# Linear attention and a cosine feed-forward layer: two more chunks paired, and Strassen's seven products in the second product of the pairs

## The chip, the core and the metric

One core of a Trainium2 chip runs the whole kernel. The metric is the time of one execution in microseconds (us) on the device. TensorE (PE) does matrix products, VectorE (DVE) and ScalarE (ACT) work elementwise, GpSimd (POOL) does a little of the attention, and SyncE (SP) issues nearly all transfers between the device memory (DRAM) and the core's buffers.

## The reference

```python
def phi(x):                                   # 64 -> 256 features
    proj = einsum('bhsd,df->bhsf', x, w_phi)
    proj = proj - max(abs(proj), axis=-1)
    return concatenate([exp(proj), exp(-proj)])
q_p, k_p = phi(q), phi(k)                     # 8 batches, 8 heads, 576 rows of 64
kv, z = einsum('bhsf,bhsd->bhfd', k_p, v), sum(k_p, axis=2)
attn = einsum('bhsf,bhfd->bhsd', q_p, kv) / (einsum('bhsf,bhf->bhs', q_p, z) + 1e-6)
x = attn as (4608 tokens, 512)
h = x @ w_in                                  # 512 x 2048
g = h * cos(h)
out = g @ w_out                               # 2048 x 512
```

The two weights arrive as float64. The kernel turns each into a high and a low part of float32; each number of x and g is split the same way, and a product of two split matrices is three products: high by high, low by high, high by low.

## The kernel before, in words

Thirty-two attention units (two heads each, `attention(u)`) write x, transposed, into `xs` and `xs_tail` in DRAM. `convert(kind, i)` makes the eight pairs of weight tiles `wi` (columns of w_in, 256 of the 2048 each) and `wo` (the same rows of w_out) and stores them to `wi_parts` and `wo_parts`. The feed-forward layer goes by chunks of 512 tokens: chunks 0 to 7 are the first 512 tokens of a batch, chunk 8 (`TAIL`) gathers the last 64 of each.

- Chunks 0 to 2 take the plain product (L969: for each tile of 128 hidden columns twelve matmuls of 512 columns), a quarter of the weights at a time, with running sums in DRAM, while the attention still runs.
- Chunks 3, 4, 5 and 6 are a `visit()` each. There the first product is Strassen's: the chunk is cut into halves of 256 tokens, the weight pair into 2 x 2 blocks, and seven block products of 256-column matmuls (L921) take the place of eight. `fold`, during chunk 3, makes the block sums of w_in that this needs. ACT copies products out of PSUM (L933), DVE adds them up (L948, L952). Then g = h cos(h) is made (ACT L991 and L999, DVE L995 and L1002), split by ACT (`gh`, L49) and DVE (`gl`, L54), and taken through the second product at once: L1018 to L1020, twelve matmuls of 512 columns a tile, with g stationary and w_out moving.
- The last two chunks, 8 and 7, go as a pair in `visit_two()`: Strassen's first product with whole chunks as halves, so its matmuls have 512 columns (L1196), 42 to a weight pair. The second product is plain (L1311 to L1313): chunk 8's at once, chunk 7's from g that was kept in buffers the attention no longer needs.

Weight pairs are read back from DRAM by `reload` where they have left their ring of buffers: three buffers for `wi`, three for `wo`.

Every instruction belongs to a `Step`, and a table of step numbers, `ORDER`, sets the order; each engine executes its own steps in that order. A step waits for the steps it depends on and for its buffers. PSUM has eight banks, given out by the same order.

Of the kernel before, what the change touches and what calls it, by code (L numbers as in the profile page):

```python
# [7 lines left out]
F32 = mybir.dt.float32  # L8
# [13 lines left out]
NSLOT = 4  # L22


@with_exitstack
def phi_attention_then_cos_ffn(ctx: ExitStack, tc: tile.TileContext, qkT, vS, w_phi, w_in, w_out, out):
# [8 lines left out]
    T = out.shape[0]  # L35
# [32 lines left out]
    class Step:  # L68
# [18 lines left out]
    ORDER = [  # L87
# [206 lines left out]
    ]  # L294
    LATENCY = dict(PE=0.35, ACT=0.25, DVE=0.2, POOL=0.25, SP=2.0)

    def plan():
# [511 lines left out]
    def visit(v):  # L809
# [94 lines left out]
        for i, pr in enumerate(pairs):  # L904
# [3 lines left out]
            if c == GROUP:  # L908
                w_fold[wi]()
# [548 lines left out]
```

## Time and profile before

| | before |
|---|---|
| median of 3 runs | 1032.85 us (1032.52 to 1035.78) |
| span of the profiled execution | 1030.4 us |
| PE busy | 1021.3 us (99%) |
| DVE busy | 760.7 us (74%) |
| ACT busy | 780.0 us (76%) |
| POOL busy | 147.1 us (14%) |
| moved by transfers | 193.39 MB |

The profile is of one execution, whose whole time isn't given apart from its span; the span is 2.45 us shorter than the median of the runs. Busy time is the time in which an engine had at least one instruction under way.

### The profile page before, as it was taken

Reading aid. Unit: us, or ns where it says so; the run is one execution under the profiler, and the core shown is the slowest. Engines: PE = TensorE matmul, PEld = TensorE weight load, DVE = VectorE, ACT = ScalarE, POOL = GpSimd, SP = SyncE. Lnnn points to the kernel's source line nnn. Section 1 sums busy time; section 2 is a strip of 40 time slices with the busy share of each in tenths; the row PEclk is TensorE's granted clock in tenths of the full one; section 3 lists DMA queues with packets and bytes.
Section 4 is the critical chain, followed back from the end, with each engine's and each line's share of the span. In section 5 each row is a group of like instructions: output and inputs, shape, how many; then the busy total and the mean of one; then the engine's idle time right before and its main releaser. Section 6 shows DMA issues by size and latency. Waiting matters only on the chain.

```text
span 1030.4 us, 23501 instructions
## 1 busy us (share of the span) xinstructions
PE 1021.3 (99%) x9402; PEld 862.9 (84%) x9402; DVE 760.7 (74%) x1426; ACT 780.0 (76%) x1592; POOL 147.1 (14%) x231
## 2 busy tenths in 40 slices
PE   9999999999999999999999999999999999999998
PEld 6778887888888788889889898888898988888886
DVE  7999888999889878988776666666666676645532
ACT  7899987778688877975889867996788875545532
POOL 3433332020200202211111110111101100000000
PEclk9999999999999999999999999999999999999999
DMA  6655665647536556774926771477347443535134
GB/s 239 212 188 161 216 203 181 219 145 257 205 115 227 189 187 222 239 225 156 328 89 227 269 269 55 164 268 256 131 163 264 141 146 83 200 126 215 41 133 153
DMA packets 86893, 193.39 MB, mean 188 GB/s; under 512 B 20608, under 2 KB 41216, under 8 KB 82944
## 3 DMA queue, kind: packets, MB, share of 16 engines
q1 hardware_dynamic: 86640, 191.82, 55.5%
q8 instruction: 74, 1.21, 0.5%
q14 instruction: 35, 0.29, 0.1%
q10 hardware_dynamic: 144, 0.07, 0.0%
HBM read 141.52 MB, written 50.33 MB: 186 GB/s over the span
## 4 chain that ended last, share of the span: by engine, by line
PE 90%; ACT 3%; DVE 3%; DMA 2%; issue 1%; POOL 0%; SPq 0%; DVEq 0%; ACTq 0%; POOLq 0%
PE bank L921 16%; PE bank L969 10%; PE bank L1018 10%; PE bank L1019 9%; PE bank L1020 9%; PE bank L1196 8%; PE bank L747 5%; PE bank L712 5%; PE bank L1312 3%; PE bank L1311 3%; PE bank L1313 3%; PE bank L608 3%; PE bank L562 2%; PE bank L654 1%; PE bank L718 1%; ACT ek L666 1%
## 5 line engine op out<-in xcount | busy, mean ns | idle before, releaser
L1018 PE MATMUL bank<-wo,gh 128*128 128x512 f32 x448 | 178.9, 399 | 0.1
L1019 PE MATMUL bank<-wo,gh 128*128 128x512 f32 x448 | 175.1, 391 | 0.0
L1020 PE MATMUL bank<-wo,gl 128*128 128x512 f32 x448 | 175.0, 391 | 0.0
L601 POOL TENSOR_TENSOR pq<-pq,bq 128x288 f32<-128x288 f32 x128 | 119.4, 965 | 165.7 <-DVE bq L597 87.2
L666 ACT ACTIVATE ek<-bank,mk 128x128 f32<-128x128 f32 x464 | 129.0, 411 | 7.0 <-DVE mk L649 6.7
L54 DVE TENSOR_TENSOR gl<-g,gh 128x512 fp32r<-128x512 f32 x128 | 89.8, 707 | 41.1 <-ACT gh L49 39.7
L1018 PEld LDWEIGHTS bank<-wo,gh 128*128 128x128 f32 x448 | 84.3, 188 | 20.7 <-issue 3.1
L995 DVE SCALAR_TENSOR_TENSOR g<-g,hs 128x512 f32<-128x512 int32 x112 | 80.1, 721 | 29.2 <-ACT g L991 24.9
L1020 PEld LDWEIGHTS bank<-wo,gl 128*128 128x128 f32 x448 | 84.1, 188 | 19.1 <-DVE gl L54 0.8
L593 POOL COPY m<-m 32x36 f32<-32x36 f32 x96 | 26.9, 280 | 506.4 <-DVE m L588 503.8
L49 ACT ACTIVATE gh<-g 128x512 fp32r<-128x512 f32 x128 | 80.8, 637 | 23.6 <-DVE g L1002 15.5
L1019 PEld LDWEIGHTS bank<-wo,gh 128*128 128x128 f32 x448 | 84.4, 188 | 14.6
L999 ACT ACTIVATE g<-g,halfpi 128x512 f32<-128x512 f32 x112 | 79.1, 719 | 18.2 <-DVE g L995 17.7
L1002 DVE TENSOR_TENSOR g<-hs,g 128x512 f32<-128x512 f32 x112 | 77.0, 691 | 16.7 <-ACT g L999 16.4
L672 ACT ACTIVATE eq<-pq 128x576 f32<-128x576 f32 x128 | 81.4, 717 | 3.7 <-POOL pq L601 3.5
L921 PE MATMUL bank<-xh_t,wi 128*128 128x256 f32 x512 | 83.6, 285 | 0.0
L921 PEld LDWEIGHTS bank<-xh_t,wi 128*128 128x128 f32 x512 | 72.5, 191 | 4.9 <-DVE wi L54 0.8
L747 PE MATMUL bank<-kv,eq 128*64 128x65 f32 x2048 | 70.4, 223 | 3.2 <-ACT hs L977 2.5
L933 ACT ACTIVATE hs<-bank 128x256 f32<-128x256 f32 x128 | 48.1, 398 | 33.5 <-PE bank L921 31.0
L747 PEld LDWEIGHTS bank<-kv,eq 128*64 128x64 f32 x2048 | 64.7, 138 | 9.5 <-ACT hs L977 2.8
L712 PEld LDWEIGHTS bank<-vs,ek 128*64 128x64 f32 x2048 | 62.5, 138 | 5.6 <-issue 1.1
L712 PE MATMUL bank<-vs,ek 128*64 128x65 f32 x2048 | 66.1, 223 | 0.0
(144 smaller groups left out, 2235.6 us busy)
## 6 DMA issues: line engine op xcount, KB each, us to landing
wi<-wi_parts SPq DMA_DIRECT2D x20, 1792.0 KB, 8.5
wo<-wo_parts SPq DMA_DIRECT2D x30, 1024.0 KB, 6.0
qk<-qkT SPq DMA_DIRECT2D x31, 640.0 KB, 5.1
wi_parts<-wi SPq DMA_DIRECT2D x32, 512.0 KB, 6.1
x_raw<-xs SPq DMA_DIRECT2D x47, 256.0 KB, 4.6
vs<-vS SPq DMA_DIRECT2D x32, 325.0 KB, 5.4
wi_raw<-w_in SPq DMA_DIRECT2D x8, 1024.0 KB, 7.0
wo_raw<-w_out SPq DMA_DIRECT2D x8, 1024.0 KB, 6.3
```

The source lines that it names most:

```text
L54: eng.tensor_tensor(out=out, in0=in_, in1=hi.bitcast(F32), op=ALU.subtract)
L601: qeng.tensor_tensor(out=d["pq"][:, c], in0=d["pq"][:, c], in1=d["bq"][:, c], op=ALU.subtract)
L666: ACT.activation(out=e[:, g, s * P:(s + 1) * P], in_=pk[:, g, :], func=AF.Exp, scale=1.0 - 2.0 * s, bias=d["lk" if s == 0 else "mk", i][:, ...
L672: ACT.activation(out=e[:, s, :], in_=d["pq"][:, j * S:(j + 1) * S], func=AF.Exp, scale=1.0 - 2.0 * s)
L712: PE.matmul(out=acc[c:c + 64, n, i, :], lhsT=e[:, s, P * n + c:P * n + c + 64], rhs=vs[b["v"].slot][:, 2 * s + i, :], start=(s == 0 and i ...
L747: PE.matmul(out=ps[64 * h:64 * h + 64, 65 * g:65 * g + 65], lhsT=d["eq", j][:, n, c:c + 64], rhs=d["kv"][:, 2 * n + j, :], start=h not in ...
L921: PE.matmul(out=out, lhsT=w[:, part, block, j * P:(j + 1) * P], rhs=d[x, name][:, j * HC:(j + 1) * HC], start=start and k == 0, stop=k == ...
L969: PE.matmul(out=bank(b), lhsT=w[:, part, 2 * r + kt // 2, kt % 2 * P:(kt % 2 + 1) * P], rhs=d.get(("from", kt), d)[x, kt], start=(k == 0), ...
L1018: PE.matmul(out=a, lhsT=gh[:, t], rhs=w[:, 0, r], start=first, stop=False)
L1019: PE.matmul(out=a, lhsT=gh[:, t], rhs=w[:, 1, r], start=False, stop=False)
L1020: PE.matmul(out=a, lhsT=gl[:, t], rhs=w[:, 0, r], start=False, stop=last)
L1196: PE.matmul(out=bank(bank_b), lhsT=w[:, part, block, j * P:(j + 1) * P], rhs=d[x, name, j], start=start and k == 0, stop=k == 5, skip_grou ...
```

## The change

Chunks 5 and 6 become a pair, ahead of the last one, so `visit()` is left with chunks 3 and 4. In both pairs the second product goes by Strassen's seven products as well, and transposed: slices of w_out are stationary and g moves. For that all g of both chunks of a pair (8 weight pairs x 4 tiles) are kept in buffers of the attention, and then seven `sweep`s go over all eight weight pairs, each into two PSUM banks: per weight pair three matmuls for each bank. Four sweeps first combine two kept tiles on DVE (`combine`). The slices of w_out come from DRAM (`fetch`, four weight pairs in one transfer of 1 MB): three sweeps take blocks of `wo_parts`, four take block sums, `wo_sums`, which `fold_wo` makes during chunk 4. The result of the pairs leaves transposed, in an output of its own, `outT`, which the host puts in place after the run.

`wi` has two buffers instead of three; the room of the third is `wi_x`, two half tiles, which a weight pair uses in the visits and x and g use in the pairs.

```diff
-    rings.update(wi=3, wo=3, v=2, ...)
+    rings.update(wi=2, wi_x=1, wo=3, v=2, ...)
...
-    kept = NP - rings["wi"]
-    TWICE = 1
-    late = [c for c in range(GROUP, NCH) if c != NCH - 2] + [NCH - 2]
+    SINGLE = (3, 4)
+    PAIRS = ((5, 6), (TAIL, 7))
+    kept = NP - rings["wi"] - rings["wi_x"]
...
+        def fold_wo():
+            def join():
+                x["t1"] = new("w_t", [P, 2 * DM], F32, "wo_s", "w_t1")
+                hi, lo = (flat(w_tiles[me][:, n]).bitcast(F32) for n in range(2))
+                DVE.tensor_tensor(out=x["t1"], in0=hi, in1=lo, op=ALU.add)
+            def sums(k):
...
+                DVE.tensor_tensor(out=o, in0=a, in1=b, op=op)
+            def sums_high():
+                x["s"] = new("w_raw", [P, 4, 2, DM // 2], F32R, "wo_st", "w_raw")
+                hi_of(ACT, x["s"][:, :, 0], x["t1"].rearrange("p (k c) -> p k c", k=4))
+            def sums_low():
+                lo_of(DVE, x["s"][:, :, 1], x["t1"].rearrange("p (k c) -> p k c", k=4), x["s"][:, :, 0])
+            def put():
+                SP.dma_start(out=wo_sums[:, i], in_=x["s"].bitcast(F32))
...
+            if c == SINGLE[-1]:
+                w_fold[wo]()
...
-            def mm2(tbs):
-                w = w_tiles[wo]
-                for tb in tbs:
-                    t = slice(tb * P, (tb + 1) * P)
-                    a = bank(c["acc"][tb])
-                    PE.matmul(out=a, lhsT=n["gh"][:, t], rhs=w[:, 0, r], start=first, stop=False)
-                    PE.matmul(out=a, lhsT=n["gh"][:, t], rhs=w[:, 1, r], start=False, stop=False)
-                    PE.matmul(out=a, lhsT=n["gl"][:, t], rhs=w[:, 0, r], start=False, stop=last)
...
+        for i, pr in enumerate(seq):
+            m, hs, whole = products(pr)
+            for r in range(2):
+                for n in range(2):
+                    wave(i, m, hs, (r, n), whole[r, n])
+            if i < NP - rings["wi"]:
+                reload("wi", seq[rings["wi"] + i], True, True)
...
+        def combine(i, o, a, b):
+            def fn():
+                DVE.tensor_tensor(out=at[(i,) + o], in0=at[(i,) + a], in1=at[(i,) + b], op=ALU.subtract)
...
+        def sweep(k, key, out, start, form=None):
+            for half in range(2):
+                fetch(k, half)
+            for i in range(NP):
+                if form:
+                    combine(i, *form)
...
+                def mm2(js, n=n, box=box, place=place, i=i):
+                    w = box["w"]
+                    for j in js:
+                        for q, (part, x) in enumerate(((0, "gh"), (1, "gh"), (0, "gl"))):
+                            PE.matmul(out=bank(out[j]), lhsT=w[:, place, part, j * P:(j + 1) * P], rhs=n[x],
+                                      start=start and i == 0 and q == 0, stop=i == NP - 1 and q == 2, skip_group_check=True)
...
+        p1 = sweep("a01", (0, 0), X, True)
+        p5 = sweep("s2", (0, 1), Y, True, ((0, 1), (0, 1), (0, 0)))
+        p6 = sweep("s1", (0, 1), X, False, ((0, 1), (1, 1), (0, 1)))
+        p3 = sweep("s3", (1, 1), Y, False)
+        p7 = sweep("s0", (0, 0), X, False, ((0, 0), (0, 1), (0, 0)))
+        p2 = sweep("a11", (1, 0), Z, True)
+        p4 = sweep("a10", (1, 0), X, False, ((1, 0), (1, 0), (0, 1)))
...
-    ORDER = [
+    ORDER = [0, 3, 5, 4, 7, 8, 6, 9, 10, 11, 2, 42, 44, 59, 46, 47, 64, 65, 68, 45, 1, 12, 17, 19, 1265, 58, 18, 20, 16, 21, 83, 48, 22, 60, 13, 61, 14, 1266, 25,
```

Of the order the rows of three places follow. First PE's last instructions before the change, the end of the plain second product of chunk 7 (bank_N is a PSUM bank, `gh` and `gl` the halves of g):

```order
L1311 MATMUL bank_75<-wo,gh 128x512
L1312 MATMUL bank_75<-wo,gh 128x512
L1313 MATMUL bank_75<-wo,gl 128x512
L1311 MATMUL bank_71<-wo,gh 128x512
L1312 MATMUL bank_71<-wo,gh 128x512
L1313 MATMUL bank_71<-wo,gl 128x512
```

And the same end now, in the seventh sweep of the second pair:

```order
L1389 MATMUL bank_76<-gh,wo 128x512 x2
L1389 MATMUL bank_76<-gl,wo 128x512
L1389 MATMUL bank_69<-gh,wo 128x512 x2
L1389 MATMUL bank_69<-gl,wo 128x512
L1389 MATMUL bank_76<-gh,wo 128x512 x2
L1389 MATMUL bank_76<-gl,wo 128x512
```

Four banks, three matmuls each, have become two banks, three matmuls each, for twice the tokens.

Second, SP's queue where the reloads of w_in for the last pair stood before (`wi_parts`, `wo_parts` in DRAM into `wi`, `wo`; `out` takes results of chunk 6):

```order
L523 DMA wo<-wo_parts_101 128x2048
L523 DMA wi<-wi_parts_94 128x2x1792
L1078 DMA out<-o 128x512 x2
L523 DMA wi<-wi_parts_95 128x2x1792
L523 DMA wo<-wo_parts_102 128x2048
L523 DMA wi<-wi_parts_96 128x2x1792
L523 DMA wi<-wi_parts_97 128x2x1792
```

And the reloads for the pair of chunks 5 and 6 now (`xs` and `xs_tail` take results of the last attention units, L1343 is a slice of w_out):

```order
L528 DMA wi<-wi_parts_93 128x2x1792
L1343 DMA wo<-wo_parts 128x8x256
L528 DMA wi<-wi_parts_94 128x2x1792
L1343 DMA wo<-wo_parts 128x8x256
L528 DMA wi<-wi_parts_95 128x2x1792
L789 DMA xs_tail<-xt 128x64
L1062 DMA out<-o 128x512
L789 DMA xs_tail<-xt 128x64
L793 DMA xs<-xt 32x4x128 x4
L528 DMA wi<-wi_parts_96 128x2x1792
```

The reloads of a pair now stand among stores of the attention, which is still running, and the first slices of w_out are fetched between them.

Third, ACT's part of a fold. Before, only w_in was folded, and ACT wrote the high part into the resident tile `wi` (`ek`, `eq`, `pq` are the attention's, `xh_` the split x, `hs`, `g`, `gh` the feed-forward layer's):

```order
L977 ACTIVATE hs<-bank_73 128x512
L999 ACTIVATE g<-g,halfpi 128x512
L49 ACTIVATE gh<-g 128x512 x2
L49 ACTIVATE wi<-wi_s 128x1024
L999 ACTIVATE g<-g,halfpi 128x512
L976 ACTIVATE g<-bank_73 128x512
```

These folds of w_in are still there; the new ones, of w_out, write the staging buffer `wo_st`. This is the place of the last of them:

```order
L671 ACTIVATE ek<-bank_69,mk 128x128 x8
L995 ACT_TABLE_LOAD
L995 ACTIVATE g<-g,halfpi 128x512
L929 ACTIVATE hs<-bank_76 128x256
L987 ACTIVATE g<-hs 128x512
L50 ACTIVATE xh_b_8826<-x_raw 128x512
L987 ACTIVATE g<-hs 128x512
L50 ACTIVATE xh_t_8902<-x_raw 128x512
L578 ACTIVATE pq<-bank_75 128x512
L50 ACTIVATE xh_t_8929<-x_raw 128x512
L50 ACTIVATE wo_st<-wo_s 128x4x256
L578 ACTIVATE pq<-bank_70 128x512
```

The high part of the fold before that one stands four rows ahead of these; between the two, ACT works for the attention and for chunk 4.

## Rows read from the trace of the kernel before

**Rows 1.** The head of the page: the span, the engines' busy time with its share and number of instructions, and the shares of the chain that ended last.

```profile
span 1030.4 us, 23501 instructions
PE 1021.3 (99%) x9402; PEld 862.9 (84%) x9402; DVE 760.7 (74%) x1426; ACT 780.0 (76%) x1592; POOL 147.1 (14%) x231
PE 90%; ACT 3%; DVE 3%; DMA 2%; issue 1%; POOL 0%; SPq 0%; DVEq 0%; ACTq 0%; POOLq 0%
```

**Rows 2.** Busy time by stretch: the stretch, its length, busy us and instructions of PE, PE's weight loads, DVE, ACT and POOL, then the granted TensorE clock, the busy share of the transfer engines and GB/s.

```profile
0.00:500.00 500.00, 495.11 (x4998) 407.84 (x4999) 439.97 (x808) 408.65 (x834) 103.91 (x158) 1.00 0.61 201
500.00:850.00 350.00, 349.57 (x3639) 311.25 (x3639) 230.31 (x478) 286.75 (x613) 43.15 (x74) 1.00 0.57 196
850.00:1000.00 150.00, 150.00 (x653) 122.17 (x652) 82.61 (x131) 78.59 (x136) 0.00 (x0) 1.00 0.38 130
```

**Rows 3.** PE's waits over the whole span: the line that waited, what it waited for, us in total, times, longest.

```profile
PE bank L747 <- ACT hs L977: 2.5, 1, 2.5
PE bank L1405 <- DVE warm L350: 1.1, 1, 1.1
PE bank L633 <- DMA qk<-qkT: 0.5, 1, 0.5
```

**Rows 4.** Groups of instructions by line and operation: the tiles, partitions and elements, the number, busy us and mean ns of one, then idle time ahead of them.

```profile
L1018 PE MATMUL bank<-wo,gh 128*128 128x512 f32 x448 | 178.9, 399 | 0.1
L1020 PE MATMUL bank<-wo,gl 128*128 128x512 f32 x448 | 175.0, 391 | 0.0
L921 PE MATMUL bank<-xh_t,wi 128*128 128x256 f32 x512 | 83.6, 285 | 0.0
L921 PE MATMUL bank<-xh_b,wi 128*128 128x256 f32 x384 | 62.4, 285 | 0.0
L921 PE MATMUL bank<-xl_t,wi 128*128 128x256 f32 x256 | 51.4, 282 | 0.0
L921 PE MATMUL bank<-xl_b,wi 128*128 128x256 f32 x192 | 38.6, 283 | 0.0
L1313 PE MATMUL bank<-wo,gl 128*128 128x512 f32 x128 | 50.0, 390 | 0.0
```

**Rows 5.** The chain that ended last, in order of time: start, us, engine, tile and line, number of instructions in a row.

```profile
288.41 5.44 PE bank L969 x24
...
644.64 4.31 PE bank L921 x36
...
848.63 1.40 PE bank L1196 x6
...
876.37 11.10 PE bank L1196 x48
```

**Rows 6.** The order of time on PE in two stretches, one in a visit of a single chunk and one near the end: start, duration, line, operation.

```profile
575.00 0.40 PE L1018 MATMUL bank<-wo,gh 128*128 128x512 f32 x1
...
577.75 0.52 PE L921 MATMUL bank<-xh_b,wi 128*128 128x256 f32 x3
...
1010.11 0.39 PE L1311 MATMUL bank<-wo,gh 128*128 128x512 f32 x1
...
1012.83 0.39 PE L1311 MATMUL bank<-wo,gh 128*128 128x512 f32 x1
```

**Rows 7.** Groups of DVE's instructions, as in rows 4: a low part of g, a step of the cosine, and the join, the sums and the low part of a fold of w_in.

```profile
L54 DVE TENSOR_TENSOR gl<-g,gh 128x512 fp32r<-128x512 f32 x128 | 89.8, 707 | 41.1 <-ACT gh L49 39.7 <-PE bank L921 0.9
L1002 DVE TENSOR_TENSOR g<-hs,g 128x512 f32<-128x512 f32 x112 | 77.0, 691 | 16.7 <-ACT g L999 16.4
L468 DVE TENSOR_TENSOR wi_s<-wi 128x1024 f32<-128x1024 f32 x8 | 10.0, 1246 | 0.0
L475 DVE TENSOR_TENSOR wi_s<-wi_s 128x256 f32<-128x256 f32 x32 | 13.3, 416 | 0.4
L54 DVE TENSOR_TENSOR wi<-wi_s,wi 128x1024 fp32r<-128x1024 f32 x8 | 10.3, 1283 | 2.7 <-ACT wi L49 2.7
```

**Rows 8.** The order of time on DVE in a stretch without waits, four instructions that follow each other.

```profile
468.53 0.68 DVE L54 TENSOR_TENSOR gl<-g,gh 128x512 fp32r<-128x512 f32 x1
...
470.33 0.68 DVE L1002 TENSOR_TENSOR g<-hs,g 128x512 f32<-128x512 f32 x1
```

**Rows 9.** Groups of ACT's instructions: a high part of g, the high part of a fold of w_in, the loads of the sine's table.

```profile
L49 ACT ACTIVATE gh<-g 128x512 fp32r<-128x512 f32 x128 | 80.8, 637 | 23.6 <-DVE g L1002 15.5 <-PE bank L1019 4.1 <-DVE g L1278 1.9
L49 ACT ACTIVATE wi<-wi_s 128x1024 fp32r<-128x1024 f32 x8 | 8.5, 1062 | 4.9 <-DVE wi_s L475 4.9
L999 ACT ACT_TABLE_LOAD x38 | 48.8, 1283 | 0.7
```

**Rows 10.** Transfers by tiles: the queue, number, KB each and median us from issue to landing; the two last lines are for all transfers of the tile wi and of the tile wo, the stores to DRAM among them.

```profile
wi<-wi_parts SPq DMA_DIRECT2D x20, 1792.0 KB, 8.5
wo<-wo_parts SPq DMA_DIRECT2D x30, 1024.0 KB, 6.0
wo_parts<-wo SPq DMA_DIRECT2D x16, 512.0 KB, 7.3
...
DMA to landing us min/median/max: 3.0/7.6/10.6
...
DMA to landing us min/median/max: 3.7/6.2/14.9
```

**Rows 11.** The order of time at the end of the span: the last matmul and the last store.

```profile
1026.20 0.39 PE L1313 MATMUL bank<-wo,gl 128*128 128x512 f32 x1
...
1027.50 0.33 SPq L1353 DMA_DIRECT2D out<-o  x1
```

More of the change, by code (lines that the diff above doesn't have):

```diff
@@ L22, with phi_attention_then_cos_ffn @@
 NSLOT = 4
+ORDER_OF_COLUMNS = (5, 6, 8, 7)
 @with_exitstack
-def phi_attention_then_cos_ffn(ctx: ExitStack, tc: tile.TileContext, qkT, vS, w_phi, w_in, w_out, out):
+def phi_attention_then_cos_ffn(ctx: ExitStack, tc: tile.TileContext, qkT, vS, w_phi, w_in, w_out, out, outT):
     nc = tc.nc
@@ L1283, in wave @@
             s4 = Step("ACT", 0.62, cosine, [s3], use=[g], table="s", kind=stage + "cosine")
-            first = home is not None and home[2] == 0
-            deps = [s4] + ([home_first[id(home[0])]] if home is not None and not first else [])
-            s5 = Step("DVE", 0.61, times, deps, take=[home[0]] if first else [],
-                      use=[g, hs[key]] + ([home[0]] if home is not None and not first else []), port=True, kind=stage + "times")
-            if first:
-                home_first[id(home[0])] = s5
@@ L1362, in visit_two @@
-        A, B = ({"acc": [Buf("bank") for _ in range(NB3)], "done": {}, "before": None} for _ in range(2))
-        left = {}
-        todo = list(pairs) if not resident else list(pairs[rings["wo"]:])
-        if not resident:
-            for _ in range(rings["wo"]):
-                reload("wo", todo.pop(0))
-        for i, pr in enumerate(pairs):
+            if h.ring == "wi_x":
+                s5 = claim("wi_x", Step("DVE", 0.61, times, [s4], use=[g, hs[key]], port=True, kind=stage + "times"))
+            else:
+                old = h.first
+                s5 = Step("DVE", 0.61, times, [s4, old], take=[] if old else [h.b], use=[g, hs[key]] + ([h.b] if old else []), port=True,
+                          kind=stage + "times")
+                h.first = h.first or s5
@@ L1376, in visit_two @@
-            if i < kept:
-                reload("wi", pairs[rings["wi"] + i])
-                reload("wo", todo.pop(0))
-        finish(A, cs[0], False)
-        back = pairs[kept:] + pairs[:kept]
-        for i, pr in enumerate(back):
-            for r in range(2):
-                n, b, st = left[pr, r]
-                end = i == len(back) - 1 and r == 1
-                apply(B, n, "kept", b, pr, r, st, i == 0 and r == 0, end, end and last_visit)
-            if i < kept:
-                reload("wo", back[rings["wo"] + i])
@@ new lines, in visit_two @@
+        X, Y, Z = ([Buf("bank") for _ in range(2)] for _ in range(3))
+        before = None
+        readers = {k: [] for k in wrote}
+        def combine(i, o, a, b):
+            def fn():
+                DVE.tensor_tensor(out=at[(i,) + o], in0=at[(i,) + a], in1=at[(i,) + b], op=ALU.subtract)
+            ks = [(i,) + v for v in (o, a, b)]
+            st = Step("DVE", 0.61, fn, wrote[ks[1]] + wrote[ks[2]] + wrote[ks[0]] + readers[ks[0]], use=list(dict.fromkeys(kept_in[v] for v in ks)),
+                      port=True, kind=stage + "g_sum")
+            for v in ks[1:]:
+                readers[v].append(st)
+            wrote[ks[0]] = [st]
+            readers[ks[0]] = []
@@ new lines, in visit_two, with column, put, fn @@
+        free, ends = {}, {}
+        def column(n):
+            c = cs[n]
+            first = sum(2 for x in PAIRS[:number]) * CT + n * CT
+            return slice(first, first + CT)
+        def put(tile_of, p, n, j, deps, b):
+            def fn():
+                SP.dma_start(out=outT[p * 2 * P + j * P:p * 2 * P + (j + 1) * P, column(n)], in_=tile_of())
+            Step("SP", 0.36, fn, deps, use=[b], kind=stage + "out_store", pipe=0.75)
+        kept_c = {}
+        def take_out(name, ring, src, dep):
+            out = []
+            for j in range(2):
+                b = Buf(ring)
+                def fn(j=j):
+                    t = kept_c[name, j] = new(ring, [P, CT], F32, ring)
+                    ACT.activation(out=t, in_=bank(src[j]), func=AF.Copy, scale=1.0)
+                out.append((b, Step("ACT", 0.5, fn, dep, take=[b], use=[src[j]], kind=stage + "snap")))
+            return out
@@ new lines, in add_to, with fn @@
+        def add_to(name, src, dep, there, p, n):
+            out = []
+            for j in range(2):
+                b, old = there[j]
+                def fn(j=j):
+                    t = kept_c[name, j]
+                    DVE.tensor_tensor(out=t, in0=bank(src[j]), in1=t, op=ALU.add)
+                st = Step("DVE", 0.61, fn, dep + [old], use=[src[j], b], kind=stage + "even")
+                put(lambda j=j: kept_c[name, j], p, n, j, [st], b)
+                out.append(st)
+            return out
@@ new lines, in visit_two, with left, right @@
+        p7 = sweep("s0", (0, 0), X, False, ((0, 0), (0, 1), (0, 0)))
+        odd = add_to("cd", X, [p7], cd, 0, 1)
+        p2 = sweep("a11", (1, 0), Z, True)
+        add_to("ca", Z, [p2], ca, 1, 0)
+        free[id(X)] = odd
+        p4 = sweep("a10", (1, 0), X, False, ((1, 0), (1, 0), (0, 1)))
+        if not final:
+            for j, (b, st) in enumerate(take_out("c0", "o", X, [p4])):
+                put(lambda j=j: kept_c["c0", j], 0, 0, j, [st], b)
+            return
+        for j in range(2):
+            b = Buf("o")
+            def left(j=j):
+                t = kept_c["c0", j] = new("o", [P, CT], F32, "o")
+                ACT.activation(out=t[:, 0:HC], in_=bank(X[j])[:, 0:HC], func=AF.Copy, scale=1.0)
+            def right(j=j):
+                DVE.tensor_copy(out=kept_c["c0", j][:, HC:CT], in_=bank(X[j])[:, HC:CT])
+            s1 = Step("ACT", 0.27, left, [ends[j,]], take=[b], use=[X[j]], kind=stage + "out_copy")
+            s2 = Step("DVE", 0.34, right, [ends[j,], s1], use=[X[j], b], kind=stage + "out_copy")
+            put(lambda j=j: kept_c["c0", j], 0, 0, j, [s1, s2], b)
@@ L1441, in _arrange, with _assemble @@
             "w_out": np.ascontiguousarray(inputs["moe_w_out"]).view(np.int64)}
+def _assemble(rows, columns, B, S):
+    import numpy as np
+    done = np.empty((B, S, rows.shape[1]), rows.dtype)
+    n = rows.shape[0] // CT
+    done[:n, :CT] = rows.reshape(n, CT, -1)
+    parts = columns.reshape(columns.shape[0], -1, CT).transpose(1, 2, 0)
+    for part, c in zip(parts, ORDER_OF_COLUMNS):
+        if c < B:
+            done[c, :CT] = part
+        else:
+            done[:, CT:] = part.reshape(2, B, 32, -1).transpose(1, 0, 2, 3).reshape(B, S - CT, -1)
+    return done.reshape(B * S, -1)
 def kernel(**inputs):
```

379 lines of the change are left out of this document (211 added, 168 removed), and 351 rows, old and new, of the table ORDER.

## The prediction

> **What bounds the kernel now.** I read the page's head first: TensorE (PE) is busy 1021.3 of 1030.4 us, and the chain that ended last is 90% PE [rows 1]. That mean could hide a stage with another limit, so I asked for the busy time by stretch [rows 2]: PE fills 495.11 of the first 500 us (attention beside the first chunks), 349.57 of the next 350, and all of 850 to 1000, at a granted clock of 1.00 in each, the 2.4 GHz level. So PE bounds every stretch. What it waits for is small: the largest wait is 2.5 us, and the list runs out below 0.5 us after three entries [rows 3]. Hence the time is the sum of PE's instructions, each at the step with which they follow each other. A matmul's own duration is no use for that: it is pipelined, 399 ns by the groups [rows 4], while the next one starts after 230.
>
> The steps, from stretches in which PE runs one kind without a gap. A 256-column matmul of L921: 36 in 4.31 us, 119.7 ns [rows 5]. A 512-column one of the wide first product, L1196: 48 in 11.10 us, 231.3 ns; of the first product of chunks 0 to 2, L969: 24 in 5.44, 226.7 ns [rows 5]. The second product L1018 to L1020: twelve from 575.00 to 577.75, 229.2 ns; L1311 to L1313, near the end: twelve from 1010.11 to 1012.83, 226.7 ns [rows 6]. As a cross-check, 653 matmuls of 512 columns fill 150.00 us between 850 and 1000: 229.7 ns [rows 2].
>
> **The change, part by part.**
>
> *First product of chunks 5 and 6.* The four chunks that go singly have 512 + 384 + 256 + 192 = 1344 matmuls on L921 [rows 4]; half of them, 672, go, at 119.7 ns: 80.4 us. In their place stand 336 of 512 columns, by the row of L1196 231.3 ns: 77.7 us. That part saves 2.7 us.
>
> *Second product of the four paired chunks.* L1018 to L1020 run 448 times each for seven chunks and L1311 to L1313 128 times each for two [rows 4], so a chunk has 192 matmuls. Chunks 5 and 6 lose 384 at 229.2 ns, 87.9 us; the last pair loses 384 at 226.7 ns, 87.0 us. Added are seven sweeps of eight items of six matmuls for two pairs, 672. No row has a matmul with a slice of w_out stationary and g moving. Two have weights stationary and 512 columns of split data moving, as here: L969 with 226.7 ns and L1196 with 231.3, which give 152.3 and 155.4 us. I take the first, since L969 like a sweep goes through one bank after another in order, where L1196 returns to a bank after its copy; L1311's 226.7 stands on the same side. The part saves 22.6 us, with 19.5 as the other bound.
>
> PE saves 25.3 us in all, or 22.2 by the dearer row.
>
> One rule speaks against this size. The Trainium skill, "TensorE: Matmul & The Clock Gate", section "Back-to-back issue gap", gives N/2.4 + 2.5 ns for an isolated matmul at full clock: 109 ns for 256 columns and 216 for 512, and by it the whole change would be worth 672 x 109 - 240 x 216 ns, an estimate of 21.6 us. The trace differs from it by 10 to 15 ns a matmul at either size, and the rows decide.
>
> *DVE.* Added: 64 combinations of kept g, eight of each in four sweeps of both pairs; 48 more low parts (7 x 8 splits of g a pair instead of 4 x 8); for the folding of w_out 8 joins, 32 sums and 8 lows. By the rows [rows 7]: 64 x 0.69 (as L1002) = 44, 48 x 0.707 = 34, 8 x 1.246 + 32 x 0.416 + 8 x 1.283 = 33.6; with a few additions of the results and fewer copies about 115 us. DVE goes from 760.7 to about 875, 87% of the new span. It stays beside PE where PE has enough work there. In a pair that is so: 336 + 336 matmuls are about 155 us of PE, and DVE has 204 operations for it, 123 us at the step of 0.60 that it keeps when it has nothing to wait for [rows 8], 141 at 0.69. The tightest place is a sweep with a combination: 6 matmuls are 1.36 to 1.39 us, combination and low 1.20 by the step, 1.4 by the mean, in four of seven sweeps.
>
> Before the pairs it is denser than it was: attention is squeezed into less time. Counting PE's order off at these steps, the first wide product stands at about 680 us (848.63 now [rows 5]), and DVE's order at the row means has about 607 us of work ahead of it, 89%. In the first 500 us DVE is at 440 of 500, 88%, with PE losing 4.9 us [rows 2], that is 1%; the next 350 us, with DVE at 66%, lose 0.4. If the 1% holds on from 500 to 680, that costs 1.8 us. I take 1.8 for it.
>
> *ACT.* 48 more highs of 0.637 us and 8 of 1.06, sixteen table loads of 1.28 fewer [rows 9], half of the narrow copies exchanged for half as many wide ones: with 780.0 us it stays as it is, 78%. It hides behind PE as now.
>
> *Transfers.* The slices of w_out: 28 of 1 MB instead of 20 reloads. A sweep uses one in four items, 5.5 us, with three buffers, so some 11 us from a free buffer to its next use; 1 MB lands in 6.0 us [rows 10]. Hidden, nothing charged; were it not, all 28 would pay. The reloads of w_in in the pairs have two buffers now. A weight pair's 42 wide matmuls are 9.7 us, so a reload has 9.7 us and what else the order puts between, by my count 9.7 to 11.5 in the first pair and 11 to 14 in the second; 1792 KB land in 8.5 us at the median, 10.6 at most of this tile's transfers [rows 10]. Twelve reloads; at the median nothing, at the maximum about 1 us. I charge nothing.
>
> *Folding w_out.* Eight stores of 1 MB from one staging buffer. The next high on ACT must wait for the landing of the store before it, and all later work of ACT queues behind it. 512 KB stores of w_out land in 7.3 us [rows 10]; no row has one of 1 MB, so it takes between 7.3 and the 14.9 that is this tile's maximum. By the order and the row means ACT has, in the last four places, some 7 to 9 us of other work between a store's issue and the next high. So from 0 to 3 x 6 us of ACT's time; what reaches PE is less by the g and gh that PE has in hand. I take 0.7 us and keep 0 and 6 for the range.
>
> *The end.* Last matmul at 1026.20, last store at 1027.50 [rows 11]; the changed kernel ends with the same two half copies and one store. No difference.
>
> Sum: 1030.4 - 25.3 + 1.8 + 0.7 = 1007.6 for the span. The page gives one execution; the median of the runs, 1032.85, stands 2.45 above its span, and I carry that: 1010.0 us, and by the bounds (25.3 saved and no new wait; 22.2 saved and 1.8 + 6 of waits) 1007.5 to 1018.5.
>
> **The rivals.**
>
> *New transfers set waits (17%).* For it: one staging buffer, two slots, and SP's queue, where a reload stands behind stores that wait for attention's last results. Against it: the medians above. Price: three folding stalls of 2 us and twelve reloads late by 0.5 us, 6 + 6 us less what is absorbed: 1015 to 1022.
>
> *DVE takes over before the pairs (9%).* For it: 89% busy, and what it has is in order, so each wait of its own is passed on. If DVE can't do more than the 88% at which it ran beside a full PE, 607 us take 690 instead of 680, and at 86% 706: 10 to 26 us, less the 1.8 in the sum: 1018 to 1034. Against it: no row shows PE waiting for DVE apart from the start [rows 3].
>
> *Narrow matmuls give back only their columns (8%).* If a narrow one that goes is worth half of a wide one, 113.3 ns, because its extra 6 ns fall on something else, 672 of them give 76.1 us and the saving is 21.0: 1014.3. Against it: 36 in a row at 119.7. The Trainium skill's formula cited above would come out beside this case, at 1013.7.
>
> *Slower than before, by late reloads of w_in (3%).* With two slots each of the twelve must land within about 11.5 us on the average. The gain is spent when each is 2 us late, from 13.5 us on; the longest here is 10.6 [rows 10], with the transfer engines at 57 to 61% [rows 2]. At 14 us the time would be 1010 + 12 x 2.5 = 1040. Against it: in the pairs the engines are less busy, 38% from 850 us on [rows 2].
>
> *Cheaper than I say (5%).* The row of L1018, the first matmul after a change of kind, is 8 ns longer than L1020's [rows 4]; fewer changes between narrow and wide would then give 2 to 5 us more: 1005 to 1008.
>
> **How the numbers follow.** My forecast has 58%, and its own range is 1007 to 1014. The range must leave out no more than two in ten: from 1004.5 to 1018.5 it holds the forecast, the cheaper case, the columns' case, half of the transfers' case and a little of DVE's, some 80%. A measurement of this kernel can tell 0.3%, 3.1 us, from no change. Faster by that is below 1029.7: everything but late reloads of w_in and the far end of DVE's, 0.94; within 0.3%: 0.03; slower: 0.03.
>
> **What would show it.** Right: PE still at 99% of a span near 1008; 672 matmuls left on the narrow line at 0.12, the sweeps' 672 following each other at 0.2265 to 0.2315; the first wide product near 680 us; PE's list of waits not above 8 us. Wrong, by place: PE waiting for a transfer of w_in in the pairs; ACT idle for the staging buffer ahead of the first pair, with PE behind it; PE waiting for DVE's low parts in the sweeps with combinations; or PE losing more than 1% between 300 and 680 us with DVE above 90%. A step of the sweeps that lies outside 0.2265 to 0.2315 would break the sum itself.

## The result and the profile after

The changed kernel took 1007.01 us (median of 4 runs, 1006.06 to 1007.48), the kernel before 1033.97 in the runs beside it; the ratio is 0.9737 (95% interval 0.9723 to 0.9751). The forecast was 1010.0, its range 1004.5 to 1018.5. The profiled execution's span went from 1030.4 [rows 1] to 1004.4 us, 26.0 less, where the sum had 22.8.

The head of the page of the changed kernel, to be held against [rows 1]:

```profile
span 1004.4 us, 22964 instructions
PE 993.7 (99%) x8970; PEld 827.6 (82%) x8970; DVE 877.2 (87%) x1584; ACT 797.5 (79%) x1607; POOL 159.8 (16%) x231
PE 74%; DVE 15%; ACT 6%; issue 2%; DMA 1%; SPq 1%; POOL 0%; DVEq 0%; ACTq 0%; POOLq 0%
```

PE is still busy 99% of the span. DVE has gained 116.5 us. The chain that ended last now runs through DVE for 15%, where it was 3%, although PE hardly waits. Added up by stretches, 103 of these 151 us lie in the first 200 us, where 27 did before, 19 from there to 500, 28 between 500 and 683, and 1 behind that: this is not the pairs' doing.

Busy time by stretch, columns as in [rows 2]; the first wide product stands at 687 us:

```profile
0.00:500.00 500.00, 495.28 (x5195) 406.92 (x5197) 447.67 (x820) 420.21 (x868) 113.36 (x168) 1.00 0.62 204
500.00:683.00 183.00, 181.80 (x2202) 158.70 (x2199) 167.08 (x336) 163.99 (x370) 41.33 (x56) 1.00 0.66 230
683.00:850.00 167.00, 166.46 (x921) 137.92 (x920) 143.93 (x243) 119.40 (x213) 5.07 (x7) 1.00 0.63 194
850.00:1000.00 150.00, 150.00 (x663) 124.05 (x661) 117.72 (x187) 93.50 (x158) 0.00 (x0) 1.00 0.56 183
```

Between 500 and 683 us DVE is busy for 167.08 of 183 and PE loses 1.2. In the last 150 us 663 matmuls of 512 columns fit where 653 did [rows 2]: 226 ns each instead of 229.7.

PE's longest waits, columns as in [rows 3]:

```profile
PE bank L1498 <- DVE warm L289: 1.1, 1, 1.1
PE bank L567 <- DMA qk<-qkT: 0.9, 1, 0.9
PE bank L752 <- ACT kv L729: 0.9, 1, 0.9
PE bank L917 <- DVE mk L654: 0.6, 1, 0.6
PE bank L1389 <- DVE gl L55: 0.5, 1, 0.5
```

And pieces of the chain that ended last, columns as in [rows 5]:

```profile
605.64 2.87 PE bank L917 x24
687.35 10.97 PE bank L1204 x48
739.59 12.24 PE bank L1204 x54
838.36 13.60 PE bank L1204 x60
932.20 68.01 PE bank L1389 x300
```

No wait for `wi`, `wo` or the staging buffer is among them, and all listed waits come to 6 us. A narrow matmul (L917) still takes 2.87/24 = 119.6 ns a step and a sweep's (L1389) 68.01/300 = 226.7. But a wide one (L1204) takes 12.24/54 = 226.7 ns as well, where the same code took 231.3 before [rows 5]. Of the steps in the sum this is the one that came out otherwise.

Transfers, columns as in [rows 10]; the last line is for all stores of the fold of w_out:

```profile
wi<-wi_parts SPq DMA_DIRECT2D x17, 1792.0 KB, 8.0
wo<-wo_parts SPq DMA_DIRECT2D x22, 1024.0 KB, 6.9
wo<-wo_sums SPq DMA_DIRECT2D x16, 1024.0 KB, 5.9
wo_sums<-wo_st SPq DMA_DIRECT2D x8, 1024.0 KB, 5.7
...
DMA to landing us min/median/max: 3.8/5.7/12.4
```

### The profile page after: what moved, and what is told of

It reads as the page before. It is cut to its first block, busy times and chain, and to the rows that moved or that the text cites. A ratio compares the mean times of both kernels' runs of the same rounds, so it can differ in the third digit from the quotient of the medians.

```text
span 1004.4 us, 22964 instructions
## 1 busy us (share of the span) xinstructions
PE 993.7 (99%) x8970; PEld 827.6 (82%) x8970; DVE 877.2 (87%) x1584; ACT 797.5 (79%) x1607; POOL 159.8 (16%) x231
## 4 chain that ended last, share of the span: by engine, by line
PE 74%; DVE 15%; ACT 6%; issue 2%; DMA 1%; SPq 1%; POOL 0%; DVEq 0%; ACTq 0%; POOLq 0%
PE bank L1204 15%; PE bank L1389 15%; PE bank L965 8%; PE bank L917 6%; PE bank L1014 6%; PE bank L1016 6%; PE bank L1015 6%; PE bank L752 4%; PE bank L717 3%; ACT ek L671 2%; DVE mk L651 2%; PE bank L567 2%; DVE m L584 2%; PE bank L613 2%; DVE bq L602 1%
## 5 line engine op out<-in xcount | busy, mean ns | idle before, releaser
L606 POOL TENSOR_TENSOR pq<-pq,bq 128x288 f32<-128x288 f32 x128 | 131.5, 1057 | 107.0 <-DVE bq L602 86.2
L1389 PE MATMUL bank<-gh,wo 128*128 128x512 f32 x448 | 137.9, 389 | 0.0
L1014 PE MATMUL bank<-wo,gh 128*128 128x512 f32 x320 | 128.2, 400 | 0.1
L1016 PE MATMUL bank<-wo,gl 128*128 128x512 f32 x320 | 125.1, 391 | 0.2 <-DVE gl L55 0.2
L1015 PE MATMUL bank<-wo,gh 128*128 128x512 f32 x320 | 125.0, 391 | 0.0
L1389 PEld LDWEIGHTS bank<-gh,wo 128*128 128x128 f32 x448 | 84.1, 188 | 17.4
L1389 PE MATMUL bank<-gl,wo 128*128 128x512 f32 x224 | 87.3, 390 | 0.5 <-DVE gl L55 0.5
L752 PEld LDWEIGHTS bank<-kv,eq 128*64 128x64 f32 x2048 | 63.9, 138 | 11.4 <-ACT ek L671 2.9
L1014 PEld LDWEIGHTS bank<-wo,gh 128*128 128x128 f32 x320 | 60.2, 188 | 14.4 <-issue 1.5
L1016 PEld LDWEIGHTS bank<-wo,gl 128*128 128x128 f32 x320 | 60.1, 188 | 14.1 <-DVE gl L55 0.9
L995 ACT ACTIVATE g<-g,halfpi 128x512 f32<-128x512 f32 x80 | 56.7, 721 | 16.7 <-DVE g L991 16.1
L1015 PEld LDWEIGHTS bank<-wo,gh 128*128 128x128 f32 x320 | 60.3, 188 | 10.5
L55 DVE TENSOR_TENSOR gl<-g,gh 128x512 fp32r<-128x512 f32 x80 | 58.5, 734 | 11.1 <-ACT gh L50 11.0
L50 ACT ACTIVATE gh<-g 128x512 fp32r<-128x512 f32 x80 | 51.1, 643 | 17.3 <-DVE g L998 13.3
```

Source lines behind the costliest of these rows:

```text
L606: qeng.tensor_tensor(out=d["pq"][:, c], in0=d["pq"][:, c], in1=d["bq"][:, c], op=ALU.subtract)
L752: PE.matmul(out=ps[64 * h:64 * h + 64, 65 * g:65 * g + 65], lhsT=d["eq", j][:, n, c:c + 64], rhs=d["kv"][:, 2 * n + j, :], start=h not in ...
L1014: PE.matmul(out=a, lhsT=gh[:, t], rhs=w[:, 0, r], start=first, stop=False)
L1015: PE.matmul(out=a, lhsT=gh[:, t], rhs=w[:, 1, r], start=False, stop=False)
L1016: PE.matmul(out=a, lhsT=gl[:, t], rhs=w[:, 0, r], start=False, stop=last)
L1389: PE.matmul(out=bank(out[j]), lhsT=w[:, place, part, j * P:(j + 1) * P], rhs=n[x], start=start and i == 0 and q == 0, stop=i == NP - 1 and ...
```

## The experiments

Each time stands beside runs of the kernel before in the same session; the ratios are to those. The changed kernel's own is 0.9737.

**Is the time PE's sum?** In one sweep of each pair the matmuls are issued twice.

```diff
-                        for q, (part, x) in enumerate(((0, "gh"), (1, "gh"), (0, "gl"))):
+                        times = 2 if k == "a11" else 1
+                        for q, (part, x) in enumerate(((0, "gh"), (1, "gh"), (0, "gl")) * times):
...
-                                      start=start and i == 0 and q == 0, stop=i == NP - 1 and q == 2, skip_group_check=True)
+                                      start=start and i == 0 and q == 0, stop=i == NP - 1 and q == 3 * times - 1, skip_group_check=True)
```

> The changed kernel; in one sweep of each pair (a11) the matmuls are issued twice, so that a pair has eight sweeps' matmuls instead of seven (this product is added twice, the output is not the reference's). Nothing else is added. Theory, PE's sum sets the time: 96 more matmuls of 226.7 ns, 21.8 us, 1028.8. Rival, the sweeps are held by DVE or by the slices of w_out: PE has room, and the addition is below 15 us.

Measured: 1028.48 us, ratio 0.9947 (0.9932 to 0.9962), 21.5 us more than the changed kernel. PE's sum sets the time in the pairs; the rival is out. Counted in matmuls, this is also what eight sweeps, as a plain second product needs them, would have cost.

**What is a narrow matmul worth?** The wide matmuls of the first pair are cut in two. (The start of an accumulation is then given for each half of a bank, and the sums come out changed; why was not followed up. Number, size and order of the matmuls are as said.)

```diff
-                            PE.matmul(out=bank(bank_b), lhsT=w[:, part, block, j * P:(j + 1) * P], rhs=d[x, name, j],
+                            for c in (slice(0, HC), slice(HC, CT)) if number == 0 else (slice(0, CT),):
+                                PE.matmul(out=bank(bank_b)[:, c], lhsT=w[:, part, block, j * P:(j + 1) * P], rhs=d[x, name, j][:, c],
...
```

> The changed kernel with each of the 336 wide matmuls of the first pair's first product cut into two of 256 columns, the width that chunks 5 and 6 had before; nothing else is changed. Theory, by the rows of before: 672 x 119.7 against 336 x 226.7 ns, 80.4 - 76.2 = 4.2 us more, 1011. Rival, narrow matmuls cost their columns only: 672 x 113.3, no change.

Measured: 1010.77 us, ratio 0.978 (0.9751 to 0.9809), 3.8 us more, by the medians, for 4.2. In the chain of this kernel, the stretch that the changed kernel walks in 12.24 us:

```profile
741.76 12.95 PE bank L1205 x108
```

12.95/108 = 119.9 ns. The half of a wide step would be 113.3: the 6 ns are real and the case of the columns falls. So each half of the change has a price by a run of its own: 21.5 us for the eighth sweep and 3.8 for the narrow matmuls.

**Why did the wide step fall from 231 to 227 ns?** The code of the wide product is the same in both kernels; its neighbours and the place of its operands are not. In the trace of before the steps from start to start in the longest run of wide matmuls (the 48 of [rows 5]) come back, behind the first eight, in the same eight values (230, 226, 229, 232, 240, 230, 234, 226 ns, within 1), whatever the operand; in the changed kernel nearly all are 226 or 227. First the second halves of x were put elsewhere, in the changed kernel and in the one before:

```diff
-    HOT = {"wi", "wi_x", "wo", "gh", "gl", "w_raw", "w_t", "gx"} | {f"x_{b}" for b in BLOCKS}
+    HOT = {"wi", "wi_x", "wo", "gh", "gl"} | {f"x_{b}" for b in BLOCKS}
```

> The changed kernel, with the buffers that hold the second halves of x in the pairs (w_raw, w_t, gx) taken out of the group of buffers that is laid out first, so that they lie above 140 KB of a partition instead of below; order, operations and sizes are the same. In the kernel before, the wide matmuls (L1196) followed each other at 231 ns in a pattern of eight steps that came back exactly; in the changed kernel they do at 226.7 (L1204). Theory 1, the place of the operands decides: L1204 goes back to about 231 ns, 672 x 4.5 = 3 us longer, 1010. Theory 2, the neighbours decide (the plain second product between the wide ones before, the sweeps now): L1204 stays at 226.7 and the time within 1 us of 1007.

```diff
-    HOT = {"wi", "wo", "gh", "gl"} | {f"x_{b}" for b in BLOCKS}
+    HOT = {"wi", "wo", "gh", "gl", "ek", "pq", "eq"} | {f"x_{b}" for b in BLOCKS}
```

> The kernel before, with the buffers that hold the second halves of x in its one pair (ek, pq, eq) laid out first, below 40 KB, instead of above 128 KB; nothing else is changed. Theory 1, the place decides: L1196 falls from 231 to 226.7 ns, 336 x 4.5 = 1.5 us less, and attention's matmuls, which read the same buffers, may change too. Theory 2, the neighbours decide: L1196 stays at 231 and the time is that of the kernel before within 1 us.

Measured: 1009.95 us, ratio 0.9765 (0.9738 to 0.9791), and 1031.87 us, ratio 0.9978 (0.9965 to 0.9992). The chain of the changed kernel with the halves high, in the stretches that took 12.24 and 13.60 us:

```profile
741.98 12.50 PE bank L1204 x54
841.42 13.85 PE bank L1204 x60
```

That is 231.5 and 230.8 ns, back at the old step. The chain of the kernel before with the halves low, in the stretch that took 11.10 us [rows 5]:

```profile
878.20 10.88 PE bank L1196 x48
```

That is 226.7 ns, and in that run all 336 steps are 226 or 227. So the place decides and the neighbours don't. Height had changed together with something else, though: by the built programs' addresses within a partition, w_in and the first halves of x start at 32 modulo 256 bytes in the kernel before and in e1, the second halves at 96 (of e1's four, one at 224 and one, `x_wi`, at 32); in the changed kernel and in e2 all have one remainder. The next experiment takes e1 and puts 64 bytes ahead of the second halves, so that they stay high.

```diff
+    pad = sb.tile([P, 16], F32, name="pad", tag="pad", bufs=1)
+    POOL.memset(pad, 0.0)
```

> The kernel of e1_second_halves_high (the second halves of x above 140 KB) with 64 bytes more ahead of the buffers that are laid out last, nothing else. By the built programs' addresses all operands of the wide matmuls stand at 32 modulo 128 in the changed kernel and at 96 in e2_before_halves_low (226.7 ns), while in the kernel before and in e1 the first halves and w_in stand at 32 and the second halves at 96 (231 ns). Theory 1, a common remainder modulo 128 decides: here all stand at 32, so L1204's line goes back to 226.7 ns and the time to 1007. Theory 2, the height decides: it stays at 231 to 232 ns and 1010.

Measured: 1007.68 us, ratio 0.9741 (0.9724 to 0.9757): the time of the changed kernel again, but the step is 12.34/54 = 228.5 ns in the same stretch, neither of the two forecasts. The order of time on PE shows why; the rows are the beginnings of three blocks of six matmuls, and of the one after them:

```profile
745.39 0.39 PE L1207 MATMUL bank<-xh_t,wi 128*128 128x512 f32 x1
745.61 0.40 PE L1207 MATMUL bank<-x_raw,wi 128*128 128x512 f32 x1
...
746.77 0.39 PE L1207 MATMUL bank<-xh_b,wi 128*128 128x512 f32 x1
746.99 0.39 PE L1207 MATMUL bank<-x_gx,wi 128*128 128x512 f32 x1
...
748.12 0.39 PE L1207 MATMUL bank<-xh_t,wi 128*128 128x512 f32 x1
748.35 0.40 PE L1207 MATMUL bank<-x_t,wi 128*128 128x512 f32 x1
...
749.51 0.39 PE L1207 MATMUL bank<-xh_b,wi 128*128 128x512 f32 x1
```

The block with `x_gx` takes 1.35 us, the blocks with `x_raw` and `x_t` 1.38 and 1.39. `x_gx` lies highest of all, at 218 KB, and starts at 32 modulo 256 like the first halves; `x_raw` and `x_t`, lower, start at 160. The 64 bytes made all equal modulo 128, but of these three only `x_gx` equal modulo 256. Over the whole run the mean step is 226.9 ns in blocks with `x_gx`, 226.6 with `x_wi` (at 32, low), and 230.2 with the other two, whose steps alternate between 226 and 234. So height is out, and modulo 128 was the wrong unit:

| second halves against first halves and w_in, modulo 256 | kernels | mean step of the wide matmuls |
|---|---|---|
| equal | changed kernel, e2 | 227.5, 226.7 ns |
| 128 apart for two buffers, equal for the others | e9 | 229.3 ns |
| 64 apart, one way or the other (in e1 for three buffers) | before, e1 | 232.2, 231.7 ns |

(The means go from each start to the next; those of the changed kernel, of e1 and of e9 hold some steps next to attention. An operand's effect reaches a little beyond its own block: in e1 the blocks with `x_wi`, equal to the first halves, have a mean of 228.9 ns, their first steps behind another block 231 to 233.) Two more kernels asked whether there is more to gain. The first puts the same 64 bytes into the changed kernel; the second also 96 bytes further ahead.

> The changed kernel with 64 bytes more ahead of the buffers that are laid out last (the attention's), so that these too stand at 32 modulo 128, as the feed-forward layer's operands do already. Theory 1, the remainder counts where matmuls of one kind mix it: the wide matmuls and the sweeps have one remainder already, so within 1 us of 1007. Theory 2, it counts at the changes between attention's matmuls and the others too: the second product of the visits falls from a mean of 238 ns for the first matmul, 2 us or more are gained.

```diff
+    shift = const.tile([P, 24], F32, name="shift")
+    POOL.memset(shift, 0.0)
```

> The changed kernel with the buffers moved by 96 and 160 bytes, so that the feed-forward layer's and the attention's operands all start at a multiple of 128. Theory 1, only a common remainder counts: 226.7 ns as now, within 1 us of 1007. Theory 2, a start that is a multiple of 128 spares a piece of each read: wide matmuls below 226 ns or the narrow ones below 120 (113 would be 670 x 6 = 4 us), 1003 or less.

Measured: 1006.98 us, ratio 0.9733 (0.9718 to 0.9747), and 1006.30, 0.9729 (0.9714 to 0.9743): no change that these runs can tell. The wide step is 227.5 ns in both, the narrow one stays at 120, and the first matmul of the second product in the visits at a mean of 238. For the wide matmuls equal remainders count, and which one it is (32, 96 in e2, 128 in e11) does not. For the attention these two runs settle less than they set out to: by the built programs' addresses its operands `pq` and `eq` stood 128 from the feed-forward layer's modulo 256 in both, and `qk` 64, so that one remainder for all of them was not tried.

**Is DVE hidden in the sweeps?** The combinations are left out.

```diff
-                DVE.tensor_tensor(out=at[(i,) + o], in0=at[(i,) + a], in1=at[(i,) + b], op=ALU.subtract)
+                pass
```

> The changed kernel without the 64 combinations of kept g on DVE (the sweeps use g as it was kept; the output is not the reference's). That takes about 44 us of DVE's work out of the pairs. Theory, DVE is hidden in the sweeps: 1006 to 1007, at most 1 us less. Rival, DVE holds the sweeps: 3 us less or more.

Measured: 1006.40 us, ratio 0.9731 (0.9705 to 0.9756): 0.6 us less, within the scatter. DVE holds nothing there.

**And ahead of the pairs?** Once with more of DVE's work in the folds of w_out, once with less.

```diff
-                DVE.tensor_tensor(out=x["t1"], in0=hi, in1=lo, op=ALU.add)
+                for _ in range(2):
+                    DVE.tensor_tensor(out=x["t1"], in0=hi, in1=lo, op=ALU.add)
+                for _ in range(4):
+                    DVE.tensor_tensor(out=x["t1"][:, 0:2 * P], in0=hi[:, 0:2 * P], in1=lo[:, 0:2 * P], op=ALU.add)
```

> The changed kernel with the join of each fold of w_out made twice and four pieces of it again (the same values), 8 x (1.25 + 4 x 0.42) = 23 us more of DVE's work between 525 and 680 us. In the changed kernel DVE is busy 167.08 of 183 us between 500 and 683, so about 16 us are free there. Theory, PE bounds and DVE is hidden with little to spare: the time rises by what goes over, 6 to 13 us, 1013 to 1020. Rival 1, DVE is already the bound there: 20 us or more. Rival 2, DVE has room to spare: below 2 us.

Measured: 1030.84 us, ratio 0.9968 (0.9953 to 0.9984), 23.8 us more, the number of rival 1. The whole gain is nearly gone. From the head of its page:

```profile
span 1029.3 us, 23004 instructions
PE 1005.5 (98%) x8970; PEld 835.4 (81%) x8970; DVE 900.9 (88%) x1624; ACT 798.9 (78%) x1607; POOL 160.6 (16%) x231
```

DVE has 23.7 us more to do. The first wide product starts 23.4 us later than in the changed kernel; its row here and there, columns as in [rows 6]:

```profile
710.58 0.40 PE L1207 MATMUL bank<-xh_b,wi 128*128 128x512 f32 x1
```

```profile
687.18 0.39 PE L1204 MATMUL bank<-xh_b,wi 128*128 128x512 f32 x1
```

Busy time from 500 to 690 us, columns as in [rows 2], first of this kernel and then of the changed one:

```profile
500.00:690.00 190.00, 176.13 (x1976) 153.30 (x1973) 173.02 (x339) 151.37 (x345) 41.98 (x56) 0.95 0.60 209
```

```profile
500.00:690.00 190.00, 188.80 (x2235) 164.55 (x2232) 172.27 (x346) 170.99 (x386) 41.33 (x56) 1.00 0.65 225
```

DVE is busy for 91% of these 190 us in both: the added work made the stretch ahead of the pairs longer and did not fill the rest. PE's idle time over the whole span is 1029.3 - 1005.5 = 23.8 us against 1004.4 - 993.7 = 10.7, so 13.1 more, and its busy time rose by 11.8 us for the same 8970 instructions, with a granted clock of 0.95 in these 190 us: once PE had waited it ran at the lower level for a while. Two readings fit. Either DVE had some 10 us in hand, 13.1 us went over, as the theory has it, and the clock added 11.8, a price that the theory had left out; or DVE had nothing in hand, all of its new work came out as time, and PE's slower matmuls only filled what it would have waited. The trace does not part them; the constant 91% speaks for the second.

```diff
-                DVE.tensor_tensor(out=o, in0=a, in1=b, op=op)
+                pass
```

> The changed kernel without the 32 sums of the folds of w_out on DVE (their high and low parts and stores stay; the output is not the reference's). That takes 32 x 0.42 = 13 us from DVE between 525 and 680 us, where adding 23 us made the time 24 us longer. Theory 1, PE and DVE are level there and PE holds the time when DVE gets room: PE lost 1.2 us between 500 and 683, so at most 1 to 1.5 us less, 1005.5 to 1006.5. Theory 2, DVE alone holds that stretch: 8 to 13 us less, 994 to 999.

Measured: 1006.59 us, ratio 0.9728 (0.9713 to 0.9742). Nothing comes back, although DVE has room now:

```profile
500.00:690.00 190.00, 188.70 (x2212) 164.45 (x2209) 160.42 (x314) 170.72 (x385) 39.77 (x56) 1.00 0.64 225
```

It is busy for 84% of the 190 us, and PE for as long as before. So DVE alone doesn't hold that stretch; PE does, and DVE comes level with it or up to 10 us behind.

**How far are the new transfers from being waits?** The stores of the fold, and the reloads of w_in, are made twice in a row.

```diff
-                SP.dma_start(out=wo_sums[:, i], in_=x["s"].bitcast(F32))
+                for _ in range(2):
+                    SP.dma_start(out=wo_sums[:, i], in_=x["s"].bitcast(F32))
```

> The changed kernel with each of the eight stores of the folded w_out made twice, the second behind the landing of the first, so that the staging buffer comes free after some 12 us instead of 6. In the changed kernel the next high part of ACT follows 6 to 10 us behind the last stores. Theory, it is hidden now with little to spare: ACT stalls 2 to 6 us at each of the last four, PE loses a part of that, 2 to 8 us, 1009 to 1015. Rival, PE is covered by what it has in hand: below 1 us.

Measured: 1018.34 us, ratio 0.9861 (0.9823 to 0.9898), 11.3 us more. ACT's wait for the staging buffer, columns as in [rows 3]:

```profile
ACT wo_st L50 <- DMA wo_sums<-wo_st: 11.4, 3, 5.0
```

ACT stalls three times, 11.4 us in all, within what the theory gave it. PE covers some 3 us of it: by the page's head (span 1016.3 us, PE 997.6 busy) its idle time grew by 8.0 us, to 18.7, the upper end of the 2 to 8 expected, and its busy time by 3.9. That last part was not expected, and with it the time lies above the forecast of 1009 to 1015.

```diff
-            SP.dma_start(out=tile, in_=parts)
+            for _ in range(2 if twice else 1):
+                SP.dma_start(out=tile, in_=parts)
...
-                reload("wi", seq[rings["wi"] + i], True, True)
+                reload("wi", seq[rings["wi"] + i], True, True, True)
```

> The changed kernel with each of the twelve reloads of w_in in the pairs made twice, the second behind the landing of the first, so that a weight pair is there 16 us after its buffer came free instead of 8. By my count a reload has 9.7 to 11.5 us in the first pair and 11 to 14 in the second. Theory, the reload is hidden up to that and PE waits for the rest: 12 x 16.3 less 64 and 74, 50 to 60 us, 1057 to 1067, with PE waiting for wi. Rival, the other transfers queue behind it on SP and are late too: 70 us or more, with PE waiting for wo in the sweeps as well.

Measured: 1070.14 us, ratio 1.0349 (1.0310 to 1.0387), 63 us more. PE's longest wait:

```profile
PE bank L1205 <- DMA wi<-wi_parts: 43.8, 12, 6.2
```

And the order of time on PE behind one such wait, columns as in [rows 6]:

```profile
715.13 0.47 PE L1205 MATMUL bank<-xh_b,wi 128*128 128x512 f32 x1 [4.34 <-DMA wi<-wi_parts]
715.43 0.40 PE L1205 MATMUL bank<-x_raw,wi 128*128 128x512 f32 x1
...
716.30 0.63 PE L1205 MATMUL bank<-xl_b,wi 128*128 128x512 f32 x1
716.73 0.63 PE L1205 MATMUL bank<-x_raw,wi 128*128 128x512 f32 x1
...
719.54 0.39 PE L1205 MATMUL bank<-xh_t,wi 128*128 128x512 f32 x1
719.77 0.39 PE L1205 MATMUL bank<-x_raw,wi 128*128 128x512 f32 x1
```

All twelve reloads are waited for, 0.64 to 6.18 us each and 3.65 on the average, and nothing waits for `wo`: the theory holds for the place, and SP's queue is not the matter. By some 16 us from the first issue to the second landing less 3.65 a reload has some 12.5 us, and it needs 8.0. The six waits of the first pair average 4.94 us and those of the second 2.35, so it has about 11.4 and 14 us there, the upper ends of what was counted.

The time lies above the forecast of 1057 to 1067, although PE waits for less than was forecast: the 43.8 us of waits cost 63, since PE's busy time rose by 20.2 too, to 1013.9. Behind eight of the twelve waits PE's steps are 0.43 us for a while (716.30 to 716.73), the 1.2 GHz level, before they are 0.23 again; behind the four shortest ones they are 0.22 to 0.24 from the second step on. The Trainium skill, "TensorE: Matmul & The Clock Gate", section "Back-to-back issue gap", gives N/1.2 ns at that level, 427 for 512 columns, and the trace agrees.

## Why the prediction was right, and where not

**The bound.** PE at every stretch: right, by the page after and by the eighth sweep.

**The second product.** 22.6 us were forecast from 226.7 ns a matmul of the sweeps; it is 226.7. The number was right and its reason was not: L1196's step was taken for dear because it returns to a bank after its copy. In e2 it does so at 226.7, so that this ground for the choice was luck. (384 matmuls at 229.2 ns are 88.0 us, not 87.9; the 0.1 us changes nothing.)

**The first product.** Here a term was mis-sized. 336 wide matmuls were entered at 231.3 ns, and the 336 of the last pair were left at that. Undisturbed, all 672 run at 226.7, so the part saves 80.4 - 76.2 = 4.2 us instead of 2.7, and the old ones give 1.5 us that no term had. With that PE saves 26.8 + 1.5 = 28.3 us by the steps. The span fell by 26.0, so 2.3 us went to new small losses, for which the sum had 1.8 + 0.7; by the pages' heads PE's idle time rose from 9.1 to 10.7 us, and its busy time fell by 27.6. (The two spans are of one execution each, and the four runs of the kernel before differ by up to 3 us.) The step that failed is the reading of 231.3 as the price of such a matmul, when it was that of operands laid out at unequal remainders.

**Where the number fell.** 1007.0 is the lower end of the forecast's own 1007 to 1014, and lies in the range of the cheaper case, 1005 to 1008. That case's reason holds in part: counted from start to start in the trace of before, the 672 narrow matmuls that go took 82.0 us and the 384 of the second product 89.0, changes of kind included, where the steps without them give 80.4 and 88.0. That is 2.6 us more saved. Against it the matmuls of these kinds that stay became dearer by 3.5 us; the narrow ones' mean went from 124.3 to 127.6 ns. That two terms which the sum didn't have nearly cancel is luck.

**The rule on the step.** The Trainium skill, "TensorE: Matmul & The Clock Gate", section "Back-to-back issue gap", gives 216 ns for 512 columns and 109 for 256, for an isolated matmul. No run here shows an isolated one. In the longest undisturbed runs with equal remainders the steps are 226.7 and 119.7, and the matmuls of the change are worth 26.8 us by them. By the Trainium skill's formula the estimate was 21.6.

**DVE.** 875 us forecast, 877.2 measured; hidden in the sweeps, as said. PE's loss from 500 to 683 was put at 1.8 us and is 1.2. Not seen was how near the edge is: with DVE at 91% from 500 to 690 us it is level with PE there or up to 10 us behind (e5, e12). The rival of DVE (9%) was a better one than its chance: with 23.7 us more for DVE to do the time is 1030.84, in that rival's range.

**ACT.** Called unchanged at 780; its own terms (30.6 + 8.5 - 20.5) add up to 18.6 more, and it is 797.5. Without effect.

**Transfers and the fold.** Nothing waits for them: right. Neither does ACT for the staging buffer. The store of 1 MB, for which no row stood, lands in 5.7 us at the median, less than the 7.3 taken as the lower bound, and in 12.4 at most.

**The slower case.** Its place and its point were right: PE waits for `wi` from some 12.5 us of landing on, on the average, where 11.5 had been worked out. Its price was too low, since a wait was entered at its own length and 43.8 us of waits cost 63.

**The first wide product** stands at 687 us, not 680. That was counted with clean steps, and PE is busy for 681.3 of the 687; it is in no term.

## What to carry to other kernels

Where one engine is busy 99%, add up its instructions at steps read from undisturbed runs, and before using two different steps for one shape find out what makes them differ: here 4.6 ns a matmul lay in the addresses. A full engine's next neighbour can be level with it without any wait to show it: add work to that neighbour, and take some away, to see how near it is. And a wait of TensorE costs more than its length when the clock falls behind it: 43.8 us of waits cost 63.

## What the runs showed of the hardware

- Wide fp32r matmuls whose operands start at equal remainders modulo 256 bytes follow each other in 226.7 ns. With second operands 128 bytes off the steps alternate between 226 and 234; with 64 off they go through eight values, mean 231 to 232. Height within the partition doesn't matter: 226.9 at 218 KB. Whether the second halves have to agree with the first halves or with w_in stays open, since those two always stood alike. So does why narrow matmuls take 120 ns and not 113, and whether the attention's matmuls gain by equal remainders.
- After a wait of 4.34 us some of TensorE's steps were 0.43 us, the 1.2 GHz level, and some matmuls later 0.23 again. That happened behind eight of the twelve waits for reloads, and PE's busy time was 20.2 us longer in that run. In the run with more work for DVE, where PE had lost 13.1 us more in small waits, busy time rose by 11.8; whether that made the run longer is not shown.
